# A performer attention with a feed-forward layer on one core: Omega loaded first, v in two halves, weight sums later, and a list scheduler's table of costs

## The chip, the cores and the metric

The kernel runs on one core of a Trainium2 chip. The metric is device microseconds of one launch, the median of several runs. The engines are named as the profile names them: PE (TensorE matmuls), PEld (its weight loads), DVE (VectorE), ACT (ScalarE), POOL (GpSimd) and SP (SyncE, which issues all DMAs here).

## What is computed

```python
def _attn_ref(q, k, v, omega):           # q, k, v: (8, 8, 576, 64); omega: (128, 64)
    scale = 1.0 / np.sqrt(np.sqrt(D))
    def phi(x):
        proj = np.einsum('bhsd,md->bhsm', x, omega)
        h = proj - np.sum(x * x, axis=-1, keepdims=True) / 2.0
        return np.exp(h - np.max(h, axis=-1, keepdims=True)) / np.sqrt(m)
    q_p, k_p = phi(q * scale), phi(k * scale)
    kv = np.einsum('bhsm,bhsd->bhmd', k_p, v)
    z = np.sum(k_p, axis=2)
    return np.einsum('bhsm,bhmd->bhsd', q_p, kv) / (np.einsum('bhsm,bhm->bhs', q_p, z)[..., None] + 1e-06)

def _moe_ref(x, w_in, w_out):             # x: (4608, 512); w_in: (512, 2048); w_out: (2048, 512)
    h = x @ w_in
    return np.maximum(0.01 * h, h) @ w_out
```

## The kernel before

The weights arrive as 64-bit floats, as two 32-bit words each. To keep float32 accuracy on 16-bit matmuls, most operands are split into a high and a low float16 part, scaled by a power of two found from the largest magnitude, and each product is three matmuls (high by high, high by low, low by high).

**Stages.** `omega` loads Omega, scales it (L347), takes its maximum (L348) and splits it. `values` loads one batch of v, takes its maximum in two halves (L610) and splits it. `power_of_two` (L316 to L324) takes a maximum over the 128 partitions with an all-reduce on POOL and makes the scale on DVE; it is called once for Omega, once for each of the eight batches of v (pow_v) and once for each weight matrix (pow_w). The first key batch and the first query block are computed by the class `Whole` with float32 matmuls (L571, L572 project, L674 sums over keys, L730 transposes, L756 numerators); all later ones by `Unit` with float16 parts (L514 projects, L685 to L687 sum over keys, L749 to L751 are numerators). The results of a query block of 512 tokens are normalised (L766 to L769), split (xn) and transposed by a DMA (xt).

**Weights.** `Weight.convert` turns a piece of 64-bit words (128 x 1024) into float32: ACT copies the high word scaled (L399), DVE shifts and masks (L401), PE sums the magnitudes by eight matmuls with a column of ones (`sums`, L409), DVE ors the low word in (L412), and the sign goes back either on DVE (L420) or, for the pieces that `SIGN_POOL` lists, by ACT (L415) and a product on POOL (L417). There are eight pieces for each of w1 and w2. `Weight.scale` reads all eight sums and calls `power_of_two`; `Weight.split` makes the two float16 parts of a piece.

**Feed-forward.** For each block of 512 tokens (nine blocks) there are 16 up groups (L804) and 16 down groups (L827) of twelve 128x512 matmuls, 288 groups in all. After an up group ACT applies the leaky ReLU (L811) and copies the high part, and POOL or DVE subtracts to get the low part (L292). A down group of token tile t and quarter q needs two pieces of w2 and the parts of four up groups. The PSUM bank `ffn_0` holds the sums of magnitudes until w2's scale is made; until then up groups have the two other banks.

**The order.** The program is recorded as operations with an engine (or a choice of engines), a cost, tiles read and written, a priority and a slack. `Plan.order` then runs a list schedule: it places operations by planned start, given the engines' planned times, the one port that POOL and some DVE operations hold (`port=True`), the buffers' places and SP's planned transfers, and prefers by priority at equal starts. The result is one fixed order on each engine. `PACE` and `LATER` set due times, `PRICE` weighs engines against each other in the choice, `Z_POOL` and `SPLIT_DVE` choose among forms of a step. A cost that differs from the chip's only moves the order, as in

```python
op("POOL", 0.6, lambda: nc.gpsimd.partition_all_reduce(t[:, 2:3], mx, P,
   reduce_op=bass.bass_isa.ReduceOp.absmax), r=[f"mx_{name}"], w=[key], prio=prio)
```

Of the kernel before, what the change touches and what calls it, by code (L numbers as in the profile page):

```python
# [17 lines left out]
P = 128  # L18
# [6 lines left out]
VT = 5  # L25
# [2 lines left out]


EXP_SHIFT = 10.375  # L30
SIGN_POOL = {"w1": [0, 1, 4], "w2": [2, 3, 7]}
SPLIT_DVE = {"w1": [0, 1, 7], "w2": [0, 1, 2, 4, 5, 7]}
Z_POOL = {"k": 2, "q": 2}
PACE = {"k": 13.5, "q": 9.5, "w1": 7.0, "w1s": 0, "w2": 15.5, "w2s": 23.0}
LATER = {"w1": -10.0, "w2": -190.0, "k": -5.0, "q": -110.0}
ONE = 2.0 ** 14
KV_DOWN = 2.0 ** -24
H_DOWN = 2.0 ** -15
# [21 lines left out]
class Plan:  # L60
# [48 lines left out]
    def order(self):  # L109
# [16 lines left out]
        for o in reversed(self.ops):  # L126
            hop = 4.5 if "SP" in o.ways else 0.3
            o.tail = min(way[0] for way in o.ways.values()) + hop + max((x.tail for x in after[o.number]), default=0.0)
            if o.turn_of:
                if o.turn_of in later:  # L130
                    o.tail = max(o.tail, later[o.turn_of].tail + o.pace)
                later[o.turn_of] = o
            if not o.filler and o.prio > -1.0:
                o.prio -= 1e-4 * o.tail
        open_ = [o for o in self.ops if not o.waits]
        done = []
# [93 lines left out]
def pool_(n):  # L230
    return 0.15 + n / 450
# [3 lines left out]
def performer_ffn(ctx: ExitStack, tc, qT, kT, qn, kn, vn, omT, eye, w_in, w_out, out):  # L235
# [54 lines left out]
    def low_(n, dst, a, b, engines=("DVE",), **of):  # L290

        return ways([(e, c, lambda g=g: g.tensor_tensor(dst(), a(), b(), op=ALU.subtract), True)  # L292
                     for e, c, g in (("POOL", pool_(n), nc.gpsimd), ("DVE", dve(n), nc.vector)) if e in engines], **of)

    def at(b):
        return tiles[b.kind][b.place]
# [35 lines left out]

    def omega():
        mx = one("mx_om", [P, 1])
        op("SP", 0.45, lambda: nc.sync.dma_start(out=om32(), in_=omT), w=[(whole, "om")], moved=131072)
        op("SP", 0.45, lambda: nc.sync.dma_start(out=ident, in_=eye), w=["ident"], moved=65536)

        def constants():
            nc.vector.memset(ones, 1.0)
            nc.vector.memset(shift, EXP_SHIFT)  # L340
            nc.vector.memset(minus_half(), 0.0)
            for j in range(2):
                nc.vector.memset(minus_half()[64 * j:64 * j + 64, j * M:(j + 1) * M], -0.5 * QK_SCALE ** 2)
        op("DVE", 0.6, constants, w=["ones", (whole, "half")])

        def scaled():
            nc.vector.tensor_scalar(om32(), om32(), QK_SCALE, None, op0=ALU.mult)  # L347
            nc.vector.tensor_reduce(mx, om32(), axis=AX.X, op=ALU.max, apply_absolute_value=True)  # L348
        op("DVE", 0.8, scaled, w=[(whole, "om"), "mx_om"])
        t, key = power_of_two(mx, "om", 0)  # L350

        def split():
            nc.vector.tensor_scalar(om_c, t[:, 1:2], OM_DOWN, None, op0=ALU.mult)
            for j in range(2):
                r = slice(64 * j, 64 * j + 64)
                a = om32()[r, j * M:(j + 1) * M]
                nc.vector.tensor_scalar(om[r, 0, :], a, t[r, 0:1], None, op0=ALU.mult)
                nc.vector.scalar_tensor_tensor(om[r, 1, :], a, t[r, 0:1], om[r, 0, :], op0=ALU.mult,
                                               op1=ALU.subtract)
        op("DVE", 1.3, split, r=[(whole, "om"), key], w=["om", "om_c"], prio=0.005)  # L360


    class Weight:
# [26 lines left out]
        def convert(self, i, prio):  # L390
# [7 lines left out]

            op("ACT", act(1150), lambda: nc.scalar.activation(at(f), high().bitcast(F32), AF.Copy, scale=2.0 ** -112),  # L399
               r=[b], w=[f], prio=prio)  # L400
            op("DVE", dve(1024), lambda: nc.vector.tensor_scalar(shifted(), bits(), 3, 0x7FFFFFF8,  # L401
               op0=ALU.logical_shift_left, op1=ALU.bitwise_and), r=[f], w=[tmp], prio=prio)


            def sums():
                mag = at(tmp).bitcast(BF16).rearrange("p (a b) -> p a b", b=2)[:, :, 1]
                for c in range(8):
                    col = self.col0 + 4 * (8 * (i // 4) + c) + i % 4
                    nc.tensor.matmul(at(self.sums)[:, col:col + 1], mag[:, c * P:(c + 1) * P], ones, start=True,  # L409
                                     stop=True)  # L410
            op("PE", 0.3, sums, r=[tmp, "ones"], w=[(self.sums, self.name, i)], prio=prio)
            op("DVE", stt(1024), lambda: nc.vector.scalar_tensor_tensor(shifted(), low(), 29, shifted(),  # L412
               op0=ALU.logical_shift_right, op1=ALU.bitwise_or), port=True, r=[b], w=[tmp], prio=prio)
            if i in SIGN_POOL[self.name]:
                op("ACT", act(1130), lambda: nc.scalar.activation(at(f), high().bitcast(F32), AF.Sign), r=[b], w=[f],  # L415
                   prio=prio)
# [184 lines left out]
    def values(b, prio):  # L601
# [1 line left out]

        raw, both = buf("v"), buf("v") if b else None
        half = HP * VT
        op("SP", 0.45, lambda: nc.sync.dma_start(out=at(raw), in_=vn[b].rearrange("p (g d) -> p g d", d=E)), w=[raw],
           prio=prio, moved=P * HP * VT * 2 * E * 4)
        mx2, mx = one(f"mx2_v{b}", [P, 2]), one(f"mx_v{b}", [P, 1])
        for j in range(2):
            op("DVE", dve(half * D), lambda j=j: nc.vector.tensor_reduce(mx2[:, j:j + 1],  # L610
               at(raw)[:, j * half:(j + 1) * half, :D], axis=AX.XY, op=ALU.max, apply_absolute_value=True), r=[raw],
               w=[f"mx2_v{b}{j}"], prio=prio)
        op("DVE", 0.17, lambda: nc.vector.tensor_reduce(mx, mx2, axis=AX.X, op=ALU.max),
           r=[f"mx2_v{b}0", f"mx2_v{b}1"], w=[f"mx_v{b}"], prio=prio)
# [3 lines left out]
        lo = lambda: at(both).bitcast(F16)[:, :, :].rearrange("p a b -> p (a b)")[  # L618
            :, HP * VT * 2 * E:HP * VT * 2 * (E + D)].rearrange("p (g d) -> p g d", d=D)
        if b:  # L620
            op("POOL", 0.4, lambda: nc.gpsimd.tensor_copy(hi()[:, :, D:], at(raw)[:, :, D:]), r=[raw],
               w=[(both, "ones")], prio=prio)
        for j in range(2):
            s = slice(j * half, (j + 1) * half)
            x = lambda s=s: at(raw)[:, s, :D]
            high(half * D, x, x, lambda: t[:, 0:1], r=[key, raw], w=[(raw, j)], prio=prio)
            if not b:
                continue
            high(half * D, lambda s=s: hi()[:, s, :D], x, r=[(raw, j)], w=[(both, j)], prio=prio)
            low_(half * D, lambda s=s: lo()[:, s], x, lambda s=s: hi()[:, s, :D], r=[(raw, j), (both, j)],  # L630
                 w=[(both, 2 + j)], prio=prio)
# [14 lines left out]
    def key_batch(b, prio):  # L646
# [6 lines left out]
        for hp in range(HP):  # L653
# [14 lines left out]
            if not b:  # L668
                def sums(u=u, acc=acc, hp=hp, parts=parts):
                    for j in range(2):  # L670
                        o = at(acc)[:, (2 * (hp % 2) + j) * E:(2 * (hp % 2) + j + 1) * E]
                        for t in range(VT):
                            p = u.p()[:, 2 * t + j] if t < 4 else u.p_edge()[:, j]
                            nc.tensor.matmul(o, p, parts()[:, hp, t, j], start=(t == 0), stop=(t == VT - 1))  # L674
                op("PE", 10 * 0.12, sums, r=[u.ph, u.p32, v, (v, 0), (v, 1)], w=[acc], prio=prio)
            else:
                def sums(u=u, edge=edge, acc=acc, hp=hp, parts=parts):
                    vh, vl = parts()
# [30 lines left out]
    def query_block(j, prio):  # L709

        for hp in range(HP):
# [11 lines left out]
            else:  # L723
                qp32 = lambda qp=qp: at(qp).rearrange("p a b t -> p (a b t)").bitcast(F32)
                for i in range(2):
                    turned = buf("ffn")

                    def turn(u=u, turned=turned, i=i):
                        for g in range(4):
                            nc.tensor.transpose(at(turned)[:, g * P:(g + 1) * P], u.p()[:, 4 * i + g, :], ident)  # L730
                    op("PE", 4 * 0.12, turn, r=[u.ph, "ident"], w=[turned], prio=prio)
                    high(512, lambda qp32=qp32, i=i: qp32()[:, 512 * i:512 * i + 512], lambda turned=turned: at(turned),
                         psum=True, r=[turned], w=[(qp, i)], prio=prio)
            x, xn = buf("x"), buf("xn")
            for i in range(2):
# [180 lines left out]
```

## Time and profile before

| | us |
|---|---|
| runs (median, lowest, highest) | 1011.98, 1011.9, 1013.39 |
| profiled execution, its own time | 1012.59 |
| its span | 1010.8 |
| PE busy in it | 936.8 (93%) |
| DVE busy | 584.3 (58%) |
| ACT busy | 532.8 (53%) |
| POOL busy | 254.5 (25%) |
| mean granted TensorE clock | 0.965 of full speed |

Busy PE is not PE at its peak, since matmuls are pipelined. DVE has work for the first 760 us or so; from there the program is feed-forward groups alone.

### The profile page before, as it was taken

Reading aid. Unit: us, or ns where it says so; the run is one execution under the profiler, and the core shown is the slowest. Engines: PE = TensorE matmul, PEld = TensorE weight load, DVE = VectorE, ACT = ScalarE, POOL = GpSimd, SP = SyncE. Lnnn points to the kernel's source line nnn. Section 1 sums busy time; section 2 is a strip of 40 time slices with the busy share of each in tenths; the row PEclk is TensorE's granted clock in tenths of the full one; section 3 lists DMA queues with packets and bytes.
Section 4 is the critical chain, followed back from the end, with each engine's and each line's share of the span. In section 5 each row is a group of like instructions: output and inputs, shape, how many; then the busy total and the mean of one; then the engine's idle time right before and its main releaser. Section 6 shows DMA issues by size and latency. Waiting matters only on the chain.

```text
span 1010.8 us, 16588 instructions
## 1 busy us (share of the span) xinstructions
PE 936.8 (93%) x6616; PEld 507.4 (50%) x6616; DVE 584.3 (58%) x1145; ACT 532.8 (53%) x758; POOL 254.5 (25%) x248
## 2 busy tenths in 40 slices
PE   4973679989899998999999999999999999999998
PEld 4872335555455554555455555555444444444443
DVE  5978878989588887789678898776300000000000
ACT  5666677657664685457755686476204303402410
POOL 0122344013330243115320351033204302401410
PEclk9985898999989999999999999999999999999999
DMA  9544433695366743667266737752420110000000
GB/s 349 187 129 135 159 88 69 121 189 105 57 116 168 151 90 88 136 132 162 59 148 141 140 67 138 145 115 44 94 43 11 32 31 22 1 21 21 1 11 32
DMA packets 216428, 99.73 MB, mean 99 GB/s; under 512 B 174112, under 2 KB 206624, under 8 KB 214304
## 3 DMA queue, kind: packets, MB, share of 16 engines
q1 hardware_dynamic: 216352, 98.69, 42.0%
q8 instruction: 51, 0.84, 0.3%
q14 instruction: 25, 0.20, 0.1%
HBM read 46.50 MB, written 9.44 MB: 55 GB/s over the span
## 4 chain that ended last, share of the span: by engine, by line
PE 79%; DVE 3%; issue 2%; DMA 2%; ACT 1%; POOL 1%; SPq 0%; ACTq 0%; POOLq 0%
PE ffn L827 36%; PE ffn L804 33%; PE pj L514 5%; DMA t<-z 1%; PE mi L749 1%; PE mi L687 1%; PE mi L751 1%; PE mi L685 1%; PE mi L750 1%; PE mi L686 1%; ACT v L286 0%; DVE st L520 0%; DVE ph L292 0%; DMA qp<-ph 0%; ACT big L286 0%
## 5 line engine op out<-in xcount | busy, mean ns | idle before, releaser
L804 PE MATMUL ffn<-xt,wt 128*128 128x512 f16 x1728 | 395.0, 388 | 4.1 <-DMA xt<-xn 3.2
L827 PE MATMUL ffn<-wt,big 128*128 128x512 f16 x1728 | 386.2, 380 | 0.0
L804 PEld LDWEIGHTS <-wt 128*128 128x128 f16 x1728 | 169.2, 100 | 205.4 <-issue 19.9
L292 POOL TENSOR_TENSOR big<-row,big 128x512 f16<-128x512 f32 x144 | 181.8, 1267 | 345.3 <-ACT big L286 298.5
L827 PEld LDWEIGHTS <-big 128*128 128x128 f16 x1728 | 165.8, 98 | 190.2 <-issue 1.9
L811 ACT ACTIVATE row<-ffn 128x512 f32<-128x512 f32 x144 | 85.1, 593 | 116.9 <-PE ffn L804 80.3
L286 ACT ACTIVATE row<-ffn,s 128x512 f32<-128x512 f32 x36 | 24.6, 685 | 163.2 <-PE ffn L827 162.9
L292 POOL TENSOR_TENSOR xn<-x,xn 128x512 f16<-128x512 f32 x36 | 44.1, 1224 | 244.4 <-ACT xn L286 176.4
L531 ACT ACTIVATE p<-p,shift 128x1024 f32<-128x1024 f32 x72 | 74.4, 1035 | 43.3 <-DVE p L528 43.2
L286 ACT ACTIVATE big<-row 128x512 f16<-128x512 f32 x144 | 89.6, 625 | 2.3
L292 DVE TENSOR_TENSOR ph<-p,ph 128x1024 f16<-128x1024 f32 x60 | 80.2, 1343 | 12.7 <-ACT ph L286 12.6
L520 DVE TENSOR_REDUCE st<-pj 128x8 f32<-128x1024 f32 x72 | 77.7, 1083 | 9.6 <-PE pj L514 9.3
L514 PE MATMUL pj<-om,t 128*128 128x128 f16 x1008 | 69.6, 226 | 13.9 <-DMA t<-z 7.5
L528 DVE SCALAR_TENSOR_TENSOR p<-pj,sc,st 128x1024 f32<-128x1024 f32 x72 | 81.5, 1139 | 0.1
L514 PEld LDWEIGHTS <-t 128*128 128x128 f16 x1008 | 62.4, 101 | 21.9 <-DMA t<-z 8.6
L286 ACT ACTIVATE ph<-p 128x1024 f16<-128x1024 f32 x60 | 62.7, 1048 | 0.5
L477 ACT ACTIVATE z<-nat 128x512 f32<-128x512 f32 (+1 forms) x60 | 38.6, 645 | 40.4 <-DMA t<-z 22.9
L769 DVE TENSOR_TENSOR x<-mi,r 128x256 f32<-128x256 f32 x72 | 30.1, 419 | 50.2 <-POOL xn L292 49.0
L479 DVE TENSOR_REDUCE sq<-z 128x8 f32<-128x512 f32 (+1 forms) x60 | 42.1, 705 | 21.3 <-ACT z L477 20.8
L286 ACT ACTIVATE z<-nat,sc 128x512 f16<-128x512 f32 (+1 forms) x52 | 38.3, 738 | 14.4 <-DVE sc L487 14.3
L500 DVE SCALAR_TENSOR_TENSOR z<-nat,sc,z 128x512 f16<-128x512 f32 (+1 forms) x52 | 43.9, 850 | 3.2 <-ACT z L286 3.2
L286 ACT ACTIVATE xn<-x 128x512 f16<-128x512 f32 x36 | 22.4, 623 | 34.8 <-DVE x L769 28.1
(107 smaller groups left out, 943.6 us busy)
## 6 DMA issues: line engine op xcount, KB each, us to landing
v<-vn SPq DMA_DIRECT2D x8, 1300.0 KB, 6.1
out<-row SPq DMA_DIRECT2D x36, 256.0 KB, 2.2
big<-w_in SPq DMA_DIRECT2D x8, 1024.0 KB, 7.1
big<-w_out SPq DMA_DIRECT2D x8, 1024.0 KB, 5.3
nat<-qn SPq DMA_DIRECT2D x32, 256.0 KB, 3.2
nat<-kn SPq DMA_DIRECT2D x16, 256.0 KB, 3.2
nat<-kn SPq DMA_DIRECT2D x12, 320.0 KB, 3.4
nat<-kT SPq DMA_DIRECT2D x4, 320.0 KB, 3.8
```

Source lines behind the costliest of these rows:

```text
L286: ("ACT", act(n, int(pointer)), lambda: nc.scalar.activation(dst(), src(), AF.Copy, scale=1.0 if scale is None else value()), False),
L292: return ways([(e, c, lambda g=g: g.tensor_tensor(dst(), a(), b(), op=ALU.subtract), True) for e, c, g in (("POOL", pool_(n), nc.gpsimd), ...
L477: op("ACT", act(n), lambda: nc.scalar.activation(square(), flat(at(nat)[:, :nt, :]), AF.Square, scale=SQ_SCALE), r=[nat], w=[z], prio=prio)
L479: op("DVE", dve(n), lambda: nc.vector.tensor_reduce(at(self.sq)[:, :2 * nt], square().rearrange("p (g d) -> p g d", d=D), axis=AX.X, op=AL ...
L500: op("DVE", stt(n) + 0.15, lambda: nc.vector.scalar_tensor_tensor(zl(), heads(), up(), zh(), op0=ALU.mult, op1=ALU.subtract), port=True, r ...
L514: nc.tensor.matmul(pv()[:, g], at(self.t)[:, g0 + g, :], om[:, w, :], start=(w == 0), stop=(w == 1))
L520: op("DVE", dve(n * M), lambda: nc.vector.tensor_reduce(row(0), pv(), axis=AX.X, op=ALU.max), r=[pj], w=[st], prio=prio)
L528: op("DVE", dve(n * M), lambda: nc.vector.scalar_tensor_tensor(p(), pv(), down(), row(2).rearrange("p (g o) -> p g o", o=1).broadcast_to([ ...
L531: op("ACT", act(n * M, 1), lambda: nc.scalar.activation(flat(p()), flat(p()), AF.Exp, bias=shift), w=[p32], r=["ones"], prio=prio)
L804: nc.tensor.matmul(at(ph), wk[wp][:, c:c + P], xt[:, xp, :], start=(i == 0), stop=(i == 3 * KT - 1))
L811: op("ACT", act(512), lambda ph=ph, g=g: nc.scalar.activation(at(g), at(ph), AF.Prelu, scale=H_DOWN, alpha=0.01), r=[ph], w=[g], prio=top)
L827: nc.tensor.matmul(at(po), part(f, gp)[:, t * P:(t + 1) * P], wf[wp], start=(f == 0 and gp == wp), stop=(f == FT - 1 and gp == 1))
```

## The change

Five things are changed. Omega's load, the constants and the scaling get a priority ahead of everything else, so SP issues Omega first. Each batch of v is loaded by two DMAs of half its size, and each half's maximum waits for its own half alone. In `convert` the low word is ored in before the magnitudes are summed, and the sums get a slack of 6 us in the plan (their value is the same: the bits added lie in the low half word, which the sums don't read). The plan's costs are set anew: the float32 matmuls of the first batch cost about twice as much in it, L401 is planned shorter and as holding the port. And the tables at the top are replaced: ten pieces instead of six get their sign on POOL, other pieces are split by the short form, three batches instead of two use the longer form of z.

```diff
-SIGN_POOL = {"w1": [0, 1, 4], "w2": [2, 3, 7]}
-SPLIT_DVE = {"w1": [0, 1, 7], "w2": [0, 1, 2, 4, 5, 7]}
-Z_POOL = {"k": 2, "q": 2}
-PACE = {"k": 13.5, "q": 9.5, "w1": 7.0, "w1s": 0, "w2": 15.5, "w2s": 23.0}
-LATER = {"w1": -10.0, "w2": -190.0, "k": -5.0, "q": -110.0}
+SIGN_POOL = {"w1": [0, 1, 2, 4, 6, 7], "w2": [1, 3, 6, 7]}
+SPLIT_DVE = {"w1": [0, 1, 2, 4, 5, 6], "w2": [2, 3, 4]}
+Z_POOL = {"k": 3, "q": 3}
+PACE = {"k": 13.5, "q": 5.5, "w1": 6.5, "w1s": 4.5, "w2": 17.0, "w2s": 35.5}
+LATER = {"w1": 10.0, "w2": -280.0, "k": -45.0, "q": -165.0}
...
-    PRICE = {"PE": 1.0, "ACT": 1.2, "DVE": 20.96, "POOL": 1.0, "SP": 1.0}
+    PRICE = {"PE": 1.0, "ACT": 2.2, "DVE": 8.5, "POOL": 1.0, "SP": 1.0}
...
-        op("SP", 0.45, lambda: nc.sync.dma_start(out=om32(), in_=omT), w=[(whole, "om")], moved=131072)
+        op("SP", 0.45, lambda: nc.sync.dma_start(out=om32(), in_=omT), w=[(whole, "om")], moved=131072, prio=-0.9)
...
-            op("DVE", dve(1024), lambda: nc.vector.tensor_scalar(shifted(), bits(), 3, 0x7FFFFFF8,
-               op0=ALU.logical_shift_left, op1=ALU.bitwise_and), r=[f], w=[tmp], prio=prio)
+            op("DVE", dve2(1024), lambda: nc.vector.tensor_scalar(shifted(), bits(), 3, 0x7FFFFFF8,
+               op0=ALU.logical_shift_left, op1=ALU.bitwise_and), port=True, r=[f], w=[tmp], prio=prio)
+
+            op("DVE", stt(1024), lambda: nc.vector.scalar_tensor_tensor(shifted(), low(), 29, shifted(),
+               op0=ALU.logical_shift_right, op1=ALU.bitwise_or), port=True, r=[b], w=[tmp], prio=prio)
...
-            op("PE", 0.3, sums, r=[tmp, "ones"], w=[(self.sums, self.name, i)], prio=prio)
-            op("DVE", stt(1024), lambda: nc.vector.scalar_tensor_tensor(shifted(), low(), 29, shifted(),
-               op0=ALU.logical_shift_right, op1=ALU.bitwise_or), port=True, r=[b], w=[tmp], prio=prio)
+            op("PE", 0.3, sums, r=[tmp, "ones"], w=[(self.sums, self.name, i)], prio=prio,
+               slack=6.0)
...
-        op("SP", 0.45, lambda: nc.sync.dma_start(out=at(raw), in_=vn[b].rearrange("p (g d) -> p g d", d=E)), w=[raw],
-           prio=prio, moved=P * HP * VT * 2 * E * 4)
+        for j in range(2):
+            s = slice(j * half, (j + 1) * half)
+            op("SP", 0.45, lambda s=s: nc.sync.dma_start(out=at(raw)[:, s], in_=vn[b].rearrange("p (g d) -> p g d",
+               d=E)[:, s]), w=[(raw, j)], prio=prio, moved=P * HP * VT * E * 4)
...
-                op("PE", 10 * 0.12, sums, r=[u.ph, u.p32, v, (v, 0), (v, 1)], w=[acc], prio=prio)
+                op("PE", 10 * 0.235, sums, r=[u.ph, u.p32, (v, 0), (v, 1)], w=[acc], prio=prio)
...
-                    op("PE", 4 * 0.12, turn, r=[u.ph, "ident"], w=[turned], prio=prio)
+                    op("PE", 4 * 0.28, turn, r=[u.ph, "ident"], w=[turned], prio=prio)
...
-                    op("PE", 4 * 0.12, num32, r=[(qp, i), (kvs["32"], hp | 1)], w=[acc], prio=prio)
+                    op("PE", 4 * 0.26, num32, r=[(qp, i), (kvs["32"], hp | 1)], w=[acc], prio=prio)
```

Lines of the changed file stand up to four below those before: the all-reduce stays L316, the magnitude sums are L412, the or of the low word L404, POOL's sign product L419, the up group L808, the down group L831.

**What moves, on SP at the start of the program.** `xt_112<-omT` is Omega, `nat` a tile of k, `v_101` the first batch of v, `big` raw weights. Before:

```order
L552 DMA nat_82<-kT 128x640
L606 DMA v_101<-vn 128x2600
L335 DMA xt_112<-omT 128x256
L384 DMA big_78<-w_in 128x2048
L552 DMA nat_83<-kT 128x640
L384 DMA big_79<-w_in 128x2048
```

Now:

```order
L335 DMA xt_112<-omT 128x256
L554 DMA nat_82<-kT 128x640
L610 DMA v_101<-vn 128x1300 x2
L554 DMA nat_83<-kT 128x640
L384 DMA big_78<-w_in 128x2048
L384 DMA big_79<-w_in 128x2048
```

Omega moves from third place, behind all of v, to first; v is in two halves, and the second tile of k comes ahead of the first weights.

**What moves, on POOL around w2's all-reduce** (`pow_w_166<-mx_w_165`). `big<-row` are low parts of the feed-forward's hidden activations (one for each up group), `wt<-wt` a sign product; an `ISA` row without tiles is the instruction that the trace calls MODIFY_POOL_CONFIG. Before:

```order
L292 TENSOR_TENSOR big_78<-row_107,big_78 128x512
L292 TENSOR_TENSOR big_78<-row_108,big_78 128x512
L292 TENSOR_TENSOR big_78<-row_106,big_78 128x512
L316 ISA
L316 ISA pow_w_166<-mx_w_165 128x1
L292 ISA
L292 TENSOR_TENSOR big_79<-row_107,big_79 128x512
```

Now:

```order
L419 TENSOR_TENSOR wt_65<-wt_73,wt_65 128x1024
L292 TENSOR_TENSOR big_80<-row_106,big_80 128x512
L292 TENSOR_TENSOR big_80<-row_107,big_80 128x512
L292 TENSOR_TENSOR big_80<-row_108,big_80 128x512
L292 TENSOR_TENSOR big_81<-row_106,big_81 128x512
L292 TENSOR_TENSOR big_81<-row_107,big_81 128x512
L316 ISA
L316 ISA pow_w_166<-mx_w_165 128x1
L419 ISA
L419 TENSOR_TENSOR wt_61<-wt_73,wt_61 128x1024
L292 TENSOR_TENSOR big_81<-row_108,big_81 128x512
```

Four of the first block's low parts stood ahead of the all-reduce; now fourteen do, of up groups 1 to 14, and three sign products of w2; the last sign product stands right behind it.

## Rows read from the trace of the kernel before

**Rows 1.** Windows: start and end; length, busy us (instructions) by engine; granted clock, DMA.

```profile
66.00:99.00 33.00, 12.63 (x72) 8.88 (x72) 28.03 (x45) 22.98 (x25) 4.99 (x6) 0.55 0.38 114
99.00:130.00 31.00, 21.59 (x139) 10.30 (x139) 25.02 (x29) 18.38 (x23) 11.86 (x7) 0.82 0.50 167
130.00:166.00 36.00, 30.76 (x181) 16.00 (x180) 26.74 (x48) 24.79 (x40) 14.84 (x16) 0.91 0.31 82
166.00:234.00 68.00, 63.71 (x565) 35.10 (x563) 62.47 (x128) 46.11 (x60) 13.52 (x14) 0.95 0.65 134
234.00:760.00 526.00, 511.01 (x4173) 279.51 (x4171) 389.28 (x813) 313.40 (x452) 140.47 (x141) 0.98 0.54 111
```

**Rows 2.** Waits of PE: total us, times, longest.

```profile
PE ffn L409 <- DVE wt L401: 19.1, 6, 8.6
```

**Rows 3.** Timeline of PE around the first up groups: start, us, what.

```profile
91.74 4.00 PE L804 MATMUL ffn<-xt,wt 128*128 128x512 f16 x9
98.98 5.61 PE L804 MATMUL ffn<-xt,wt 128*128 128x512 f16 x15 [3.24 <-DMA xt<-xn]
```

**Rows 4.** Chain that ended last, in order of time: start, us, what.

```profile
165.13 0.03 PE mi L686
...
166.01 2.59 PE ffn L827 x12
...
200.03 0.89 PE pj L514 x16
...
226.59 9.42 PE ffn L804 x36
...
882.23 41.44 PE ffn L827 x192
```

**Rows 5.** Timeline of all engines from the start.

```profile
0.72 0.40 SPq L552 DMA_DIRECT2D nat<-kT  x1
...
1.64 0.42 SPq L335 DMA_DIRECT2D xt<-omT  x1
...
3.74 0.74 ACT L553 ACTIVATE z<-nat 128x640 f32<-128x640 f32 x1 [1.74 <-DMA nat<-kT]
...
10.79 1.22 PE L571 MATMUL pj<-xt,nat 128*128 128x256 f32 x2 [10.79 <-DVE xt L347]
...
16.48 1.56 DVE L576 TENSOR_REDUCE st<-pj 128x8 f32<-128x1024 f32 x2 [1.02 <-PE pj L572]
```

**Rows 6.** Timeline of DVE, around the weights.

```profile
29.10 2.79 DVE L401 TENSOR_SCALAR wt<-wt 128x1024 uint32<-128x1024 uint32 x1
...
67.20 0.15 DVE L320 TENSOR_SCALAR pow_w<-pow_w 128x1 uint32<-128x1 uint32 x1 [3.64 <-POOL pow_w L316]
...
88.68 0.69 DVE L401 TENSOR_SCALAR wt<-wt 128x1024 uint32<-128x1024 uint32 x1
...
91.36 2.35 DVE L412 SCALAR_TENSOR_TENSOR wt<-big,wt 128x1024 uint32<-128x1024 uint32 x2
...
104.81 1.23 DVE L412 SCALAR_TENSOR_TENSOR wt<-big,wt 128x1024 uint32<-128x1024 uint32 x1 [6.13 <-PE ffn L409]
```

**Rows 7.** Timeline of POOL, around products and all-reduces.

```profile
28.99 2.35 POOL L417 TENSOR_TENSOR wt<-wt,wt 128x1024 f32<-128x1024 f32 x1 [1.23 <-ACT ph L580]
...
94.08 1.78 POOL L292 TENSOR_TENSOR xn<-x,xn 128x512 f16<-128x512 f32 x1 [8.83 <-issue]
...
129.49 0.41 POOL L316 PARTITION_ALL_REDUCE pow_w<-mx_w  x1 [6.30 <-DVE mx_w L433]
...
136.97 1.15 POOL L292 TENSOR_TENSOR big<-row,big 128x512 f16<-128x512 f32 x1 [7.08 <-issue]
...
488.98 0.41 POOL L316 PARTITION_ALL_REDUCE pow_v<-mx_v  x1 [5.79 <-issue]
```

**Rows 8.** Source line of the all-reduce: who waited for it (us, times).

```profile
  DVE pow_v L320: 17.4, 4
```

**Rows 9.** DMA issues: what, number, median us from issue to landing.

```profile
xt<-xn SPq DMA_TRANSPOSE x36, 3.2
```

More of the change, by code (lines that the diff above doesn't have):

```diff
@@ L132, in order @@
                 later[o.turn_of] = o
-            if not o.filler and o.prio > -1.0:
+            if not o.filler and o.prio > -0.9:
                 o.prio -= 1e-4 * o.tail
@@ L292, in low_ @@
         return ways([(e, c, lambda g=g: g.tensor_tensor(dst(), a(), b(), op=ALU.subtract), True)
-                     for e, c, g in (("POOL", pool_(n), nc.gpsimd), ("DVE", dve(n), nc.vector)) if e in engines], **of)
+                     for e, c, g in (("POOL", pool_(n), nc.gpsimd), ("DVE", stt(n), nc.vector)) if e in engines], **of)
     def at(b):
@@ L343, in constants @@
                 nc.vector.memset(minus_half()[64 * j:64 * j + 64, j * M:(j + 1) * M], -0.5 * QK_SCALE ** 2)
-        op("DVE", 0.6, constants, w=["ones", (whole, "half")])
+        op("DVE", 1.0, constants, w=["ones", (whole, "half")], prio=-0.9)
         def scaled():
@@ L348, in scaled @@
             nc.vector.tensor_reduce(mx, om32(), axis=AX.X, op=ALU.max, apply_absolute_value=True)
-        op("DVE", 0.8, scaled, w=[(whole, "om"), "mx_om"])
+        op("DVE", 0.8, scaled, w=[(whole, "om"), "mx_om"], prio=-0.9)
         t, key = power_of_two(mx, "om", 0)
@@ L610, in values @@
             op("DVE", dve(half * D), lambda j=j: nc.vector.tensor_reduce(mx2[:, j:j + 1],
-               at(raw)[:, j * half:(j + 1) * half, :D], axis=AX.XY, op=ALU.max, apply_absolute_value=True), r=[raw],
+               at(raw)[:, j * half:(j + 1) * half, :D], axis=AX.XY, op=ALU.max, apply_absolute_value=True), r=[(raw, j)],
                w=[f"mx2_v{b}{j}"], prio=prio)
@@ L620, in values @@
         if b:
-            op("POOL", 0.4, lambda: nc.gpsimd.tensor_copy(hi()[:, :, D:], at(raw)[:, :, D:]), r=[raw],
+            op("POOL", 0.4, lambda: nc.gpsimd.tensor_copy(hi()[:, :, D:], at(raw)[:, :, D:]), r=[(raw, 0), (raw, 1)],
                w=[(both, "ones")], prio=prio)
@@ L625, in values @@
             x = lambda s=s: at(raw)[:, s, :D]
-            high(half * D, x, x, lambda: t[:, 0:1], r=[key, raw], w=[(raw, j)], prio=prio)
+            high(half * D, x, x, lambda: t[:, 0:1], r=[key], w=[(raw, j)], prio=prio)
             if not b:
```

## The prediction, made before the change was timed

> **What bounds the kernel now.** I read the windows first, then PE's waits, then the timelines of the engines that PE waited for, and the chain last. The chain gives prices at the full clock: 192 feed-forward matmuls take 41.44 us, so a group of twelve takes 2.59; sixteen projections take 0.89, one 0.056; a matmul of 65 columns takes 0.03 [rows 4]. By these prices the 288 groups are 746 us, the 1008 projections 56 and the 1704 matmuls of some 65 columns 51; with about 60 us for the float32 matmuls and sums of the start (an estimate from their spacing), PE's work is some 915 us of the profiled span of 1010.8. So 96 us are PE's idle and half-clock time, and the windows show where [rows 1]: 12.6 of 33 us busy between 66 and 99 at a granted clock of 0.55, 21.6 of 31 before 130, 30.8 of 36 before 166. From 234 to 760 PE is busy 511 of 526 us.
>
> The kernel is thus bound by PE from about 166 us on, and before that by the chain that brings it its first groups. The first up group starts at 91.74 and stops after nine matmuls for the last xt, which lands at 98.98 [rows 3]; POOL made its low part only at 94.08, after 8.83 us in which it did nothing that shows, between an all-reduce and this [rows 7]. The magnitude sums stand in PE's order ahead of groups that could run, and cost 19.1 us of waiting [rows 2]. The 17th group, the first down group, starts at 166.01, and the 35th group ends at 226.59 + 9.42 = 236.0, the 34th so at 233.4 [rows 4].
>
> **Where I look for the difference.** I counted the matmuls in PE's two orders. Behind the 34th group they carry almost the same attention per group: ahead of group 60, 91.1 us of other PE work before and 90.2 now; ahead of group 100, 118.6 in both. So I take what the two reach at the 34th group as the gain, and the rest as equal on the mean (its spread comes below).
>
> **The change part by part.** *Omega first.* Now Omega's 128 KB is issued third, at 1.64, and the first projection waits for it until 10.79 [rows 5]. The tile of k that was issued first, at 0.72, was there 3.0 us later, at 3.74. Issued first, Omega lands near 3.7 and k half a microsecond after; with ACT's square (0.74) the projections start near 4.5. That is 6.3 us earlier; DVE's first reduction moves from 16.48 to about 10.2. V's halves only matter in that they keep up: 2.6 MB then stand behind less. Bounds of this term: 3 us (if k now lands as late as Omega did) to 7.
>
> *w1's scale.* DVE is busy 28 of 33 us in the window from 66, so its work counts. Ahead of w1's maximum the new order has more on DVE: three ors of low words (two in a row take 2.35, so 1.13 each [rows 6]), two chains of sums of squares, one exponent's subtraction, the first v scale and smaller things, 10.0 us in all. w1's scale came at 67.2; now it is 67.2 - 6.3 + 10 = 71, and 4 us more because three more sign products of POOL (six, where three stood) come ahead of the all-reduce: 75.
>
> *The first up group.* Behind an all-reduce POOL's next ordinary instruction comes 7.08 us after [rows 7]. Both remaining xn stand there now: 75 + 0.4 + 7.1 + 2.4 = 85, and a DMA transpose lands 3.2 us after its issue [rows 9], so the last xt is there near 88 to 89, where it was 98.98. The waits of PE on the sums [rows 2] go, since these stand behind groups that can run and DVE's or no longer waits for them (6.13 us of DVE at 104.81 [rows 6]).
>
> *w2's scale, which is late next.* The order of POOL shows it: fourteen low parts and three sign products now stand ahead of w2's all-reduce, where four low parts stood. The 14th up group ends at 88 + 14 x 2.59 + 8 us of projections, sums and key sums between = 132 if PE never waits. It may wait: only two PSUM banks serve up groups there, each is freed by ACT, and ACT has 74 instructions worth 54.5 us between w1's scale and that group's ReLU, some of them behind DVE. Following these waits by hand I get 141. Then ReLU, copy and low part (2.3), 6.0 us until the all-reduce (5.79 where nothing else held it [rows 7]) and 0.4: w2's scale at 141 to 150, where it was 131. POOL returns 7.1 us later for the last sign product (2.35), for which DVE now waits in its order, and twelve DVE instructions follow until the second piece of w2 is split (7 us). The first down group then starts at 158 to 166, against 166.01. I take 163, nearer the upper end, as DVE and ACT are each full there.
>
> *To the 34th group.* From there PE has 18 groups (46.6) and 9 us of attention, since more of it was done before: 55.6, against 60 in the order before. Before, 7 us were lost on that stretch at a granted clock of 0.95 [rows 1]; now at least 2.5 go for a start at half clock after idling, as at 91.74, where nine matmuls took 4.00 us [rows 3] and not 1.94; I take 5. So 163 + 55.6 + 5 = 223.6, against 233.4: **9.8 us gained**, with bounds from 158 + 58 = 216 (17 gained) to 166 + 62.7 = 229 (5 gained).
>
> *Sign products on POOL, weighed against the skill.* Four more products leave DVE (4 x 1.13 = 4.5 us) for POOL (2.35 each). A shift of 0.69 us on DVE took 2.79 while one ran beside it [rows 6, 7]; by the timelines three of the six products stretched a DVE instruction so, by 5.2 us together, 0.9 per product, so four cost 3.5 and save 4.5: nothing, inside the 4 us given above. The Trainium skill, GPSIMD Engine Reference, section Key points, says that GpSimd shares its SBUF interfaces with VectorE and contends with instructions that have two SBUF inputs or a two-port mode. By that rule every product that meets DVE's ors and shifts would hold it back; the trace agrees for three of six.
>
> *The middle.* DVE waited 17.4 us in four waits for the all-reduce of a batch of v [rows 8], since the plan prices it at 0.6 us and puts almost nothing between the maximum and its reader. In the new order 3.8, 0.6 and 0.6 us of work stand there for batches 3, 4 and 5, where 1.3, 0.4 and none stood for the three short ones before. Each can cost PE 4 to 7 us. I take no change, plus or minus 7.
>
> **Sum.** Span 1010.8 - 9.8 = 1001. The profiled execution took 1012.59, 1.8 over its span, and the median of the runs lies 0.6 below it: **1002 us**.
>
> **The rivals.** *A, w2's scale decides and it is slower.* If up groups are held up by ACT for longer (bank freed late, low part late on POOL), w2's scale slides further, and PE, with no other group in its order, stands. The point is the first down group at 233.4 - 55.6 - 5 = 172.8: later than that and the kernel loses. At 178 it is 5 us slower, 1017. For it: POOL's order, and DVE waiting for the last sign product. Against it: by 132 to 141 fourteen up groups have run, where ten had.
> *B, no such wait.* If ACT and DVE keep up, PE reaches its down groups at 150 to 155 and gains 18 to 23: 991. For it: PE's own work allows 140. Against it: the 7 us and the product behind the all-reduce.
> *C, the start buys nothing.* If DVE, not Omega, sets the pace to w1's scale, the 6.3 us vanish in waits for v and the weights: the gain shrinks to 3.5, 1008. The windows show DVE idle 5 of 33 us only, which speaks for it; that the first reduction waited for PE speaks against it.
> *D, POOL's products hold DVE.* If each of the four extra products, and not every second one, pushes DVE back by its whole length, they cost 9.4 us and not 3.5; the gain falls by 5.9 to 3.9, again 1008. For it: the shift of 2.79 us; against it: three of six products passed without. It is the rule named above taken in full.
>
> **Chances.** Forecast (4 to 16 us gained) 0.48, A 0.20, B 0.14, C 0.10, D 0.08. A measurement of this kernel can tell about 0.2%, 2 us, from no change. The forecast, B, C and D are faster, 0.80 together, but in C and D and at the forecast's lower end the middle's 7 us can take it back: 0.12 of it comes out the same, 0.02 slower. So faster 0.66, same 0.12, slower 0.22. For 8 in 10 I leave out half of B's far end and half of A's: 985 to 1019, the forecast's own bounds being 995 to 1007 with 7 more either way for the middle.
>
> **What would show it.** Right: first projection near 4.5, first up group fed without a stop from 88, no wait of PE on L412, all-reduce of w2 between 141 and 150, first down group near 163, 34th group ended near 224. Wrong: a first down group after 173, a new long wait of DVE for POOL's product or of PE for ACT, or new stops behind 234 of more than the 15 us idle that stand there now.

## The result, and the profile of the changed kernel

The change makes the kernel slower. The median of six runs is 1020.18 us (1016.11 to 1021.28), that of the kernel before 1011.94 (1011.12 to 1013.39); the ratio is 1.0073, 95% interval 1.0054 to 1.0091. The forecast of 1002 was wrong in sign, and the time lies just past its range (985 to 1019). The profiled execution took 1021.28 us, its span is 1019.3.

The windows of the changed kernel, with the columns of [rows 1]:

```profile
66.00:99.00 33.00, 18.62 (x141) 17.13 (x140) 19.04 (x44) 18.97 (x24) 7.70 (x6) 0.70 0.39 104
99.00:130.00 31.00, 24.64 (x155) 11.73 (x154) 30.55 (x37) 25.17 (x32) 9.47 (x6) 0.72 0.62 204
130.00:166.00 36.00, 30.95 (x242) 17.07 (x241) 31.43 (x44) 27.03 (x42) 18.80 (x13) 0.95 0.36 74
166.00:234.00 68.00, 51.09 (x420) 27.76 (x418) 48.25 (x100) 41.93 (x51) 11.04 (x14) 0.85 0.44 102
234.00:760.00 526.00, 512.72 (x4219) 281.11 (x4217) 397.95 (x838) 317.99 (x463) 142.69 (x142) 0.99 0.54 113
```

From 66 to 130 us PE is busy 9.0 us more than in [rows 1], and from 234 to 760 about as much as there (1.7 us more). The loss shows in one stretch: from 166 to 234 PE is busy 51.09 us instead of 63.71, at a granted clock of 0.85 instead of 0.95. Ahead of it DVE is busy 30.55 of 31 us and then 31.43 of 36, where it had 25.02 and 26.74. The timeline of PE shows the place:

```profile
96.16 1.94 PE L760 MATMUL mi<-kv,qp 128*128 128x65 f32 x8 [13.53 <-DVE x L773]
97.89 4.04 PE L808 MATMUL ffn<-xt,wt 128*128 128x512 f16 x9
104.59 1.87 PE L808 MATMUL ffn<-xt,wt 128*128 128x512 f16 x4 [2.65 <-DMA xt<-xn]
...
163.73 0.34 PE L412 MATMUL ffn<-ones,wt 128*128 128x1 bf16 x8
...
166.32 2.75 PE L808 MATMUL ffn<-xt,wt 128*128 128x512 f16 x12
...
186.80 1.89 PE L516 MATMUL pj<-om,t 128*128 128x128 f16 x16 [13.62 <-DMA t<-z]
188.48 6.94 PE L831 MATMUL ffn<-wt,big 128*128 128x512 f16 x24
```

The first up group starts at 97.89 and is fed from 104.59 on; before it was 91.74 and 98.98 [rows 3]. The sixteenth up group ends at 166.32 + 2.75 = 169.1, and the first down group starts at 188.48, where it was 166.01 [rows 4]. In between PE has little but a wait of 13.62 us, by its row for t, the transposed z of a projection that stands ahead of the down group. POOL's timeline, from the first all-reduce to the first down group:

```profile
7.73 0.41 POOL L316 PARTITION_ALL_REDUCE pow_om<-mx_om  x1 [7.30 <-issue]
...
32.57 2.68 POOL L419 TENSOR_TENSOR wt<-wt,wt 128x1024 f32<-128x1024 f32 x1 [3.56 <-DVE wt L404]
41.83 0.41 POOL L316 PARTITION_ALL_REDUCE pow_v<-mx_v  x1 [6.58 <-issue]
49.24 2.64 POOL L419 TENSOR_TENSOR wt<-wt,wt 128x1024 f32<-128x1024 f32 x1 [7.01 <-DVE x L773]
...
75.75 2.36 POOL L419 TENSOR_TENSOR wt<-wt,wt 128x1024 f32<-128x1024 f32 x1 [4.07 <-DVE sq L481]
86.78 0.41 POOL L316 PARTITION_ALL_REDUCE pow_w<-mx_w  x1 [8.68 <-issue]
94.41 1.14 POOL L292 TENSOR_TENSOR xn<-x,xn 128x512 f16<-128x512 f32 x1 [7.22 <-ACT wt L286]
100.13 1.35 POOL L292 TENSOR_TENSOR xn<-x,xn 128x512 f16<-128x512 f32 x1 [4.58 <-issue]
...
163.62 1.16 POOL L292 TENSOR_TENSOR big<-row,big 128x512 f16<-128x512 f32 x1 [2.32 <-ACT big L286]
170.81 0.41 POOL L316 PARTITION_ALL_REDUCE pow_w<-mx_w  x1 [6.02 <-issue]
178.31 2.33 POOL L419 TENSOR_TENSOR wt<-wt,wt 128x1024 f32<-128x1024 f32 x1 [7.09 <-issue]
```

The first product or subtraction behind an all-reduce comes 7 us after it, and 6 to 9 us lie ahead of it once POOL has done other work. And DVE's timeline, at the same places:

```profile
2.84 0.29 DVE L347 TENSOR_SCALAR xt<-xt 128x256 f32<-128x256 f32 x1 [1.18 <-DMA xt<-omT]
3.16 0.42 DVE L348 TENSOR_REDUCE mx_om<-xt 128x1 f32<-128x256 f32 x1
...
13.11 1.21 DVE L578 TENSOR_REDUCE st<-pj 128x8 f32<-128x1024 f32 x1
...
42.27 0.15 DVE L320 TENSOR_SCALAR pow_v<-pow_v 128x1 uint32<-128x1 uint32 x1 [3.89 <-POOL pow_v L316]
...
49.91 3.06 DVE L404 SCALAR_TENSOR_TENSOR wt<-big,wt 128x1024 uint32<-128x1024 uint32 x1
...
77.14 0.21 DVE L432 TENSOR_REDUCE mxs_w<-ffn 128x16 f32<-128x64 f32 x1
...
87.23 0.15 DVE L320 TENSOR_SCALAR pow_w<-pow_w 128x1 uint32<-128x1 uint32 x1 [7.11 <-POOL pow_w L316]
...
154.90 1.22 DVE L404 SCALAR_TENSOR_TENSOR wt<-big,wt 128x1024 uint32<-128x1024 uint32 x1
...
164.10 0.23 DVE L435 TENSOR_REDUCE mx_w<-ffn 128x1 f32<-128x64 f32 x1 [1.38 <-PE ffn L412]
...
171.25 0.15 DVE L320 TENSOR_SCALAR pow_w<-pow_w 128x1 uint32<-128x1 uint32 x1 [4.72 <-POOL pow_w L316]
...
180.67 1.64 DVE L284 TENSOR_SCALAR wt<-wt,pow_w 128x1024 f32<-128x1024 f32 x1 [6.36 <-POOL wt L419]
...
182.90 0.69 DVE L292 TENSOR_TENSOR z<-nat,z 128x512 f16<-128x512 f32 x1
...
187.53 1.22 DVE L292 TENSOR_TENSOR wt<-wt,wt 128x1024 f16<-128x1024 f32 x1
```

Read these together. w1's scale (87.23) comes 10 us behind its maximum (77.14), since POOL's last sign product (75.75) stands right ahead of the all-reduce and the gap of 8.68 us begins only behind it. For w2 the last or of a low word (154.90) is done at 156.1, PE sums the piece at 163.73 behind five up groups, the all-reduce follows the low part of 163.62 by 6.02 us, the last sign product comes 7.09 us behind the all-reduce, and DVE has stood 6.36 us for it when it splits the first piece at 180.67. The z that PE's t is made of (182.90) and the last step of the second piece (187.53) stand behind that on DVE. That is the chain to 188.48.

### The profile page after: what moved, and what is told of

It is laid out like the page before. It is cut to its first block, busy times and chain, and to the rows that moved or that the text cites. A ratio compares the mean times of both kernels' runs of the same rounds, so it can differ in the third digit from the quotient of the medians.

```text
span 1019.3 us, 16623 instructions
## 1 busy us (share of the span) xinstructions
PE 942.4 (92%) x6616; PEld 512.0 (50%) x6616; DVE 577.7 (57%) x1146; ACT 535.6 (53%) x765; POOL 263.1 (26%) x252
## 4 chain that ended last, share of the span: by engine, by line
PE 68%; DVE 11%; issue 5%; ACT 3%; DMA 3%; POOL 1%; SPq 0%; ACTq 0%; DVEq 0%; POOLq 0%
PE ffn L831 33%; PE ffn L808 27%; PE pj L516 4%; DMA t<-z 1%; DVE p L530 1%; DVE ph L292 1%; PE mi L753 1%; DVE z L502 1%; DMA v<-vn 1%; DVE st L522 1%; PE mi L755 1%; PE mi L754 1%; DVE v L292 1%; DVE sq L481 1%; DVE wt L401 1%
## 5 line engine op out<-in xcount | busy, mean ns | idle before, releaser
L808 PE MATMUL ffn<-xt,wt 128*128 128x512 f16 x1728 | 390.6, 385 | 3.5 <-DMA xt<-xn 2.7
L831 PE MATMUL ffn<-wt,big 128*128 128x512 f16 x1728 | 387.3, 381 | 0.0
L808 PEld LDWEIGHTS <-wt 128*128 128x128 f16 x1728 | 168.6, 99 | 203.4 <-issue 13.7
L831 PEld LDWEIGHTS <-big 128*128 128x128 f16 x1728 | 166.1, 98 | 191.4 <-issue 3.5
L292 DVE TENSOR_TENSOR ph<-p,ph 128x1024 f16<-128x1024 f32 x60 | 77.2, 1295 | 14.8 <-ACT ph L286 14.5
L773 DVE TENSOR_TENSOR x<-mi,r 128x256 f32<-128x256 f32 x72 | 30.1, 418 | 55.6 <-POOL xn L292 54.8
L286 ACT ACTIVATE z<-nat,sc 128x512 f16<-128x512 f32 (+1 forms) x43 | 31.6, 734 | 27.1 <-DVE sc L489 27.0
L502 DVE SCALAR_TENSOR_TENSOR z<-nat,sc,z 128x512 f16<-128x512 f32 (+1 forms) x44 | 37.9, 866 | 1.9 <-ACT z L286 1.7
```

The source lines that it names most:

```text
L286: ("ACT", act(n, int(pointer)), lambda: nc.scalar.activation(dst(), src(), AF.Copy, scale=1.0 if scale is None else value()), False),
L502: op("DVE", stt(n) + 0.15, lambda: nc.vector.scalar_tensor_tensor(zl(), heads(), up(), zh(), op0=ALU.mult, op1=ALU.subtract), port=True, r ...
L808: nc.tensor.matmul(at(ph), wk[wp][:, c:c + P], xt[:, xp, :], start=(i == 0), stop=(i == 3 * KT - 1))
L831: nc.tensor.matmul(at(po), part(f, gp)[:, t * P:(t + 1) * P], wf[wp], start=(f == 0 and gp == wp), stop=(f == FT - 1 and gp == 1))
```

## The experiments

All were compared with the kernel before, on the same chip; the ratio of the change was 1.0073. The moments come from one traced execution of each kernel, and carry a few us of their own: the all-reduce of v's second batch stands at 41.83 in the change, and at 39.34 to 43.05 in four runs that move nothing ahead of it.

**The two halves of the change.** First all but the tables, then the tables alone.

```diff
-SIGN_POOL = {"w1": [0, 1, 2, 4, 6, 7], "w2": [1, 3, 6, 7]}
+SIGN_POOL = {"w1": [0, 1, 4], "w2": [2, 3, 7]}
...
-    PRICE = {"PE": 1.0, "ACT": 2.2, "DVE": 8.5, "POOL": 1.0, "SP": 1.0}
+    PRICE = {"PE": 1.0, "ACT": 1.2, "DVE": 20.96, "POOL": 1.0, "SP": 1.0}
```

(and SPLIT_DVE, Z_POOL, PACE and LATER likewise; the second run has the opposite edit in the kernel before.)

> The changed code with the tables of before (SIGN_POOL, SPLIT_DVE, Z_POOL, PACE, LATER, PRICE). Theory W, w2's scale: in the change the first down group starts at 188.5 us because w2's all-reduce stands behind fourteen low parts on POOL and a sign product stands behind the all-reduce. With the old tables the all-reduce of w2 stands ahead of every low part, so the first down group should start at 166 us or earlier and the time be 1005 to 1013 us. Rival S, w1's scale: the 8 us were lost by the first up group, which was fed 5.6 us later because an all-reduce of a batch of v stands ahead of w1's. It still stands there with the old tables, so S expects 1016 to 1021 us. Rival M, the middle: the loss lies behind 234 us, and the tables move it by less than 2 us.

> The code of before with the tables of the change. W: w2's all-reduce stands behind eleven low parts and a sign product stands right behind it, so the first down group starts at 180 us or later and the time is 1016 us or more. S: here the all-reduce of v's second batch and w1's follow each other on POOL without an ordinary instruction of weight between, so w1's scale comes near 70 us as before and the time is 1008 to 1013 us.

Old tables in the new code: 1023.44 us, ratio 1.0113 (1.0085 to 1.0141). Both theories missed. w2's all-reduce does stand early, so early that it is ahead of the last xn, which POOL makes only when it is back (POOL's timeline), and PE waits 15.8 us for the xt made from it:

```profile
72.01 0.41 POOL L316 PARTITION_ALL_REDUCE pow_w<-mx_w  x1 [5.95 <-issue]
72.30 0.42 POOL L625 CAST v<-v 128x40 f16<-128x40 f32 x1
...
132.15 0.41 POOL L316 PARTITION_ALL_REDUCE pow_w<-mx_w  x1 [6.00 <-issue]
140.24 1.14 POOL L292 TENSOR_TENSOR xn<-x,xn 128x512 f16<-128x512 f32 x1 [7.69 <-issue]
```

New tables in the old code: 1021.25, ratio 1.0089 (1.0057 to 1.0122), first down group at 195.25, as W said; w1's scale at 71.06 did not help. So neither half is better than the kernel before, and in each of the three slow orders something that PE waits for (xn, a sign product) stands behind an all-reduce on POOL. It is not all that is late: with the old tables w2's sums stand ahead of the first up group (125.36) on PE, which waits there some 23 us in eight waits for the ors ahead of sums.

**One instruction moved.** From here on the plan's order is kept, and single operations are moved in their engine's queue, ahead of or behind another or by a number of places; the queues are then merged so that each operation comes behind those that it needs:

```diff
-        for o in plan.order():
+        for o in moved(plan.order(), named):
             o.run()
...
+MOVES = [('w2 product 7', 'ahead', 'w2 reduce')]
...
+MOVES = [('w1 product 7', 'behind', 'w1 reduce')]
```

> The change with one instruction moved: POOL's last sign product of w2 goes from right behind w2's all-reduce to right ahead of it; every other engine's order is the same. W: w2's scale comes up to 2.5 us later (173 instead of 171 us), but DVE's wait of 6.4 us for the product goes, the first down group starts at 181 to 184 us instead of 188.5, and the time falls by 3 to 7 us, to 1013 to 1017. S and M: the time stays within 2 us of the change's 1020.

> The change with one instruction moved: POOL's last sign product of w1 goes from right ahead of w1's all-reduce to right behind it. w1's scale should come at 78 to 80 us instead of 86.8, the last xt near 98 instead of 104.6. S: all of these 6 us are kept to the end, 1013 to 1015 us. W: up groups start 6 us earlier, but the first down group starts at 185 us or later because low parts, last sum and all-reduce of w2 keep their order, and at most 3 us reach the end, 1017 to 1020 us.

w2's product first: 1014.69 us, ratio 1.0034 (1.0012 to 1.0055); w2's scale at 173.39, the first down group at 183.27. w1's product behind: 1014.35, ratio 1.0018 (0.9998 to 1.0038); w1's scale at 76.10, w2's at 164.40 (6.9 earlier), the first down group at 181.51; 3 of the 11 us of w1's scale stand already in its maximum (74.32 instead of 77.39). Each move of one POOL instruction gives 4 to 6 us. W was right for the first; for the second S was, since w2's scale follows w1's.

**Theory H: all holds lie on one chain.** The runs are: both moves; v's second all-reduce next to w1's (`rows` are POOL's copies behind it, `power` DVE's scale); Omega alone, in the kernel before; and the first two lists together.

```diff
+MOVES = [('w2 product 7', 'ahead', 'w2 reduce'), ('w1 product 7', 'behind', 'w1 reduce')]
...
+MOVES = [('v1 reduce', 'ahead', 'w1 reduce'), ('v1 rows', 'behind', 'w1 reduce'), ('v1 rows', 'behind', 2),
+         ('v1 power', 'ahead', 'w1 power')]
...
+MOVES = [('om load', 'ahead', 2), ('om scaled', 'ahead', 'v0 half 0')]
```

> The change with both moves: the last sign product of w1 behind w1's all-reduce, the last of w2 ahead of w2's. Theory H (POOL's hold around an all-reduce lies on one chain from w1's scale over the up groups and w2's scale to the first down group): the two gains add, w2's scale comes near 166 us and the first down group starts at 175 to 178, and the time is 1007 to 1011 us, 10 to 12 below the change. Rival O (the two overlap, as PE or DVE is late next): 1013 to 1015 us.

> The change with one all-reduce moved: that of v's second batch (and DVE's scale and POOL's copies behind it) goes from 41.8 us to right ahead of w1's all-reduce, so the first 75 us have one hold of POOL instead of two and DVE does not wait 3.9 us there. H: w1's maximum comes 3 to 6 us earlier, w1's scale at 81 to 84 us instead of 86.8, and the time is 1013 to 1017 us. Rival P (the weights' pieces and the attention on DVE set w1's maximum, not the hold): w1's scale at 86 us or later, time 1018 to 1022 us, since the last sign product still stands ahead of the all-reduce.

> The kernel before with two instructions moved: Omega's load goes to SP's first place and its scaling on DVE ahead of the maxima of v; all else keeps its order. The prediction's step: PE's first projection at 4.5 us instead of 10.8 and everything behind it 6 us earlier, so 1004 to 1007 us. Rival Q: the first projection comes at 4.5 us, but DVE's first reduction stands behind Omega's split and the all-reduce of v's first batch, so it moves by 1 us only (it waited 1.02 us for PE), and the time stays within 2 us of 1011.7.

> The change with all three moves: v's second all-reduce right ahead of w1's, w1's last sign product behind them, w2's last sign product ahead of its all-reduce. H: the gains add, w1's scale at 72 to 76 us, the first down group at 171 to 175, the time 1003 to 1008 us, below the kernel before. O and P: 1009 to 1015 us, no better than the two moves.

Both moves: 1013.59 us, ratio 1.0003 (0.9978 to 1.0027). The first down group starts at 177.24, as H said, but the time is O's; the traced execution took 1010.0, the ten runs 1008.9 to 1018.9, and by the interval the run does not decide. v's all-reduce moved: 1014.40, ratio 1.0013 (0.9996 to 1.0031), w1's all-reduce at 79.76 instead of 86.78 and its scale at 80.52, a little earlier than H said: H. Three moves: 1007.03, ratio 0.9933 (0.9910 to 0.9956), w1's scale at 72.54, first down group at 172.08: H, and faster than the kernel before. In thousandths the single moves gave 3.9, 5.5 and 6.0, together 15.4; all three gave 14.0 (the single ones and the 14.0 each to within about 3, by their intervals). In the run with v's all-reduce moved, the two stand so in POOL's timeline:

```profile
79.43 0.41 POOL L316 PARTITION_ALL_REDUCE pow_v<-mx_v  x1 [8.24 <-issue]
79.76 0.43 POOL L316 PARTITION_ALL_REDUCE pow_w<-mx_w  x1
```

Omega alone: 1014.42, ratio 1.0012 (0.9991 to 1.0033), no change. PE starts early, DVE does not (timeline of all engines):

```profile
4.78 1.19 PE L571 MATMUL pj<-xt,nat 128*128 128x256 f32 x2 [4.78 <-DMA nat<-kT]
...
7.88 2.88 DVE L610 TENSOR_REDUCE mx_v<-v 128x1 f32<-128x1280 f32 x2 [4.18 <-DMA v<-vn]
...
14.93 1.23 DVE L576 TENSOR_REDUCE st<-pj 128x8 f32<-128x1024 f32 x1
```

PE's first projection is 6.0 us earlier, DVE's first reduction 1.5, since the maxima of v and Omega's split stand ahead of it: Q.

**The last sum.** Now w2's last sum is taken before three of its five up groups, with all that follows it; on its own (behind the first list of moves), and with the three moves.

```diff
+         ('w2 sums 7', 'ahead', 3), ('w2 maximum', 'ahead', 5), ('w2 product 7', 'ahead', 3),
+         ('w2 reduce', 'ahead', 3)]
```

> The change, with w2's scale alone taken earlier and w1's side left as it is: the last magnitude sum of w2 goes ahead of three of the five up groups that it stands behind on PE, w2's maximum one place ahead on DVE (in front of the z and what follows), and on POOL the last sign product and the all-reduce go ahead of the last three low parts. Theory H: w2's scale at 161 to 165 us instead of 171, the three low parts wait for POOL's return (7 us behind the all-reduce), the first down group starts at 172 to 179 us instead of 188.5, and the time is 1008 to 1013 us. Rival R (POOL is away while up groups need their low parts, so PE stops on rows and banks and nothing is gained): first down group at 184 us or later, 1014 to 1020 us, no better than the product's move alone.

> The three moves of the run before and w2's earlier sum, maximum, product and all-reduce together. H: w2's scale at 152 to 156 us instead of 161.8, the first down group at 161 to 167 instead of 172.1, the time 998 to 1004 us, below the kernel before by 0.8 to 1.4%. Rival R: as the three moves alone, 1005 to 1009 us.

On its own: 1014.58 us, ratio 1.0027 (1.0011 to 1.0043), w2's scale at 167.25 and the first down group at 186.57. With the three: 1006.49, ratio 0.9935 (0.9920 to 0.9951). w2's scale is 5.5 us earlier than with three moves (156.69) and the first down group 4.4 later (176.51). R was right. The timeline of all engines shows why, with all four moves:

```profile
146.44 3.33 POOL L419 TENSOR_TENSOR wt<-wt,wt 128x1024 f32<-128x1024 f32 x1
...
156.25 0.41 POOL L316 PARTITION_ALL_REDUCE pow_w<-mx_w  x1 [6.49 <-DVE r L771]
...
164.22 4.49 POOL L292 TENSOR_TENSOR big<-row,big 128x512 f16<-128x512 f32 x4 [7.56 <-issue]
165.39 0.60 ACT L815 ACTIVATE row<-ffn 128x512 f32<-128x512 f32 x1 [11.11 <-POOL big L292]
...
168.39 2.17 ACT L286 ACTIVATE wt<-wt,pow_w 128x1024 f32<-128x1024 f32 x2
```

There are three `row` buffers, each held until its low part is made; POOL makes none from its product (146.44) to 164.22, so ACT stands 11.11 us for a buffer, with w2's splits (168.39) queued behind.

**The low parts elsewhere, and Omega put back.**

```diff
+         ('low 0 13', 'DVE', 'w2 power'), ('low 0 13', 'ahead', 2), ('low 0 12', 'DVE', 'w2 power'),
+         ('low 0 12', 'ahead', 5), ('low 0 11', 'DVE', 'w2 power'), ('low 0 11', 'ahead', 8)]
...
+MOVES = [('om load', 'behind', 3)]
```

> The four moves of the run before, and the three low parts that then stood behind w2's all-reduce on POOL are made by DVE instead, in the stretch in which DVE waits for that all-reduce. Theory R (what the earlier all-reduce gave was taken back because ACT stood 11.1 us for a row buffer that POOL's low parts held until its return): ACT's wait goes, the first down group starts 9 to 11 us behind w2's scale as in the run with three moves, at 165 to 169 us instead of 176.5, and the time is 999 to 1004 us. Rival (something else, as the z and t of attention or PE, is late there): first down group at 172 us or later, 1005 to 1008 us.

> The change with one DMA moved: Omega's load goes back behind the first batch of v on SP; every engine's order is the same as in the change. If the start's gain is on the path: DVE's scaling of Omega at 10.4 us instead of 2.8, its first reduction near 16.6 instead of 13.1, and 3 to 4 us more at the end, 1022 to 1025. If the start buys nothing (the waits behind it take it up): 1019 to 1021. The prediction's step, 6.3 us: 1025 to 1028.

Low parts on DVE: **998.33 us**, ratio 0.9871 (0.9850 to 0.9891), the best of all, where the kernel before took 1012.55 on that chip. The timeline of all engines:

```profile
153.97 0.41 POOL L316 PARTITION_ALL_REDUCE pow_w<-mx_w  x1 [6.50 <-DVE r L770]
...
161.33 1.15 POOL L292 TENSOR_TENSOR big<-row,big 128x512 f16<-128x512 f32 x1 [6.95 <-DVE wt L292]
...
164.33 6.43 PE L831 MATMUL ffn<-wt,big 128*128 128x512 f16 x24
```

And its window, with the columns of [rows 1]:

```profile
166.00:234.00 68.00, 65.75 (x536) 34.64 (x535) 53.93 (x113) 44.20 (x60) 9.05 (x14) 1.00 0.55 120
```

The down group starts 10 us behind w2's scale, as R said, at 164.33 and in 998.33 us even a little earlier than its ranges, and from 166 to 234 PE is busy 65.75 us at the full clock. Of the 12.2 us from the run with four moves, 2.1 stand already at w1's scale (71.18 and 73.31), where the two orders are the same. The low parts on DVE were not run without the earlier sum. Omega put back behind v: 1020.17, ratio 1.0072 (1.0048 to 1.0096), the same as the change. Omega is scaled 5.3 us later (2.84 in the change), DVE's first reduction comes 2.3 later, and w1's maximum at the same time (timeline of DVE):

```profile
8.18 0.29 DVE L347 TENSOR_SCALAR xt<-xt 128x256 f32<-128x256 f32 x1 [6.52 <-DMA xt<-omT]
...
15.42 1.21 DVE L578 TENSOR_REDUCE st<-pj 128x8 f32<-128x1024 f32 x1
...
76.89 0.21 DVE L432 TENSOR_REDUCE mxs_w<-ffn 128x16 f32<-128x64 f32 x1
```

## Why the prediction was wrong

**Omega first.** The first projection was forecast for 4.5 and came at 4.28. The 6.3 us did not go on from there: DVE's first reduction came at 13.11 and not 10.2, and the run with Omega put back shows that the end gets nothing of it. The step failed where it let DVE follow PE; rival C's mechanism is what happened, though not its 1008. Nor was the wait until 10.79 Omega's alone: DVE had its scaling behind two maxima of v there (7.65 to 10.5). With Omega's load back behind v, but its scaling ahead of the maxima, it is scaled at 8.18, so some 2 of the 6.3 us were DVE's order. (A batch of v is 1.3 MB, not 2.6; no term rests on it.)

**w1's scale** is the step that failed first: forecast 75, came 87.23. I had counted the scale of v's second batch among DVE's 10 us of added work ("the first v scale") and not asked what its all-reduce, moved ahead of w1's, does to POOL: it kept POOL from its next product from 35.25 to 49.24, and DVE waiting for 3.89 us. With it moved next to w1's, w1's all-reduce came 7.0 us earlier; with the sign product behind it as well, 15.5 (71.25). I had given the three more products 4 us as work; it was the last one's place that counted: with that one alone moved, w1's scale came at 76.10, near the 75. The window that I read DVE's load from (66 to 99) lies behind w1's scale; ahead of it DVE was busy 51.15 of 66 us.

**The first up group** follows, 10 us late, and its last xt 16: 7.22 us from the all-reduce to xn, as taken from [rows 7], but the second xn, which I had right behind the first, came at 100.13, since there is one x buffer and POOL's first xn frees it (DVE waits 5.0 us for that). That is 3.9 us more, 17.4 from w1's scale to the last xt where I had 13.5. The waits on the sums did go: none of [rows 2] is left.

**w2's scale**: forecast 141 to 150, came 171.25, 84.0 us behind w1's scale where I had 66 to 75. The 14th up group's ReLU comes 57 us behind the last xt (161.40), where I had 44 to 53. I had looked for waits for ACT; what PE waits for there is DVE, twice, for the low part of the key features (waits of PE):

```profile
PE mi L691 <- DVE ph L292: 8.0, 2, 4.3
...
PE ffn L808 <- ACT row L286: 0.8, 1, 0.8
```

The chain that ended last runs through DVE for most of the time from w1's scale to 141 us (with 7.5 us of a transfer of v in it), and no move of a POOL instruction on w1's side shortened the stretch between the two scales (88.3 us with w1's product moved, 89.7 with all three moves). Which of DVE's work made it late, no run isolates. From the last sum on, my prices held (163.73 to 171.25 is 7.5 us; I had 8.7 from the fourteenth group). What I had not seen is that the sum itself stands behind five up groups while its piece lay ready at 156.1. Taken alone that cost nothing that could be won, since the row buffers that POOL frees set the next limit (1006.49 against 1007.03); with the low parts on DVE as well w2's scale and the first down group both came 7.8 us earlier than with three moves.

**From w2's scale to the first down group**: 17.2 us, and I had 17 (146 to 163). The product behind the all-reduce was priced right; a part of it could be had back by the move of one instruction.

**To the end.** The first down group came past the 172.8 us that rival A named as the point from which the kernel loses. A, to which I gave 0.20, is right in its point and in DVE's wait for the last sign product; up groups held up by ACT, its reason, did not happen. Its line would give 1012 + 188.5 - 172.8 = 1028; the time was 1020. The difference stands in two places. The 34th group ended at 240.27 + 5.34 = 245.6, 57.1 us behind the first down group, where I had 60.6: from 66 to 166 PE was busy 74.2 us where it had 65.0 [rows 1], so up to 9 us less was left for later, and the forecast (55.6 against 60) counted 4 of these. And of the 12.2 us by which that group ended later than the 233.4 before, 8.5 are left at the end, so the rest was 3.7 us shorter, inside the 7 that I gave the middle.

**The sign products** stretched some DVE instructions, as weighed: the or at 49.91 took 3.06 us, others 1.2. None of the runs isolates that; what the moves show is that the place of one product beside an all-reduce is worth 4 to 6 us.

Against the forecast, the first down group is 25.5 us late: 12.2 in w1's scale, the rest between it and w2's. What was right were prices. What was wrong in the first half was to follow one all-reduce by its hold (w2's) and not all of them, and that the moves show; in the second half it was to look for PE's waits on ACT and not on DVE, and that is read from the trace alone. The three moves together made up for both: 1007.03.

## What to carry to other kernels

An all-reduce on POOL has a price that its own row of 0.41 us doesn't show: look for the gaps ahead of it and behind it, put what others wait for on the side where it does not meet them, what is not urgent on the other, and place two all-reduces together. A scheduler that prices it at 0.6 us moves it freely, and tables tuned on such costs need not gain on the chip; no run here gave the scheduler the measured price. Before an early result is chased, ask which buffers are held while the engine that frees them is away.

## What the runs showed of the hardware

The hold belongs to the change of kind, not to the all-reduce: two in a row stand 0.33 us apart (79.43 and 79.76). A cast ran 0.29 us behind the start of an all-reduce (72.30, old tables), and copies 0.9 us behind one, as soon as DVE's scale was there (334.13 and 334.98 in the change), without the 7 us that products and subtractions of two tensors waited. The Trainium skill, GPSIMD Engine Reference, section 2.1 (Instruction dispatch), says that the first call of a freshly loaded kernel pays about 6 us with no instruction to be seen; the trace agrees with 5.6 to 6.9 us ahead of most all-reduces that waited for nothing else that shows, the program's first apart (7.3 to 8.7 ahead of seven, among them w1's in the change), and shows that the way back costs again, 6.6 to 8.3 us in most places and up to 9.4.

At the start of the program the first all-reduce came at 7.73 though its maximum was ready at 3.6; so Omega's early arrival met an engine that was not ready either.
